# Decaying attention with a soft mixture of experts on one core: fill transposes left out, the first pair of tiles reordered, two steps of the softmax moved

## The chip, the cores and the metric

One core of one Trainium2 chip. The metric is the device time of the slowest (here the only) core in microseconds, lower is better. The kernel before takes 162.74 us, the median of three runs (161.5, 162.74 and 279.86).

## The reference

Two stages, all in float32. The first is causal attention with a decay and no softmax, for 4 batches, 8 heads, 768 positions and 64 channels; `lam` is one number per head:

```python
intra = (q_b @ k_b.T * Dmask) @ v_b          # Dmask[i, j] = lam ** (i - j) for i >= j
inter = (q_b * lam ** (pos + 1)) @ kv_state
kv_state = lam ** block * kv_state + (k_b * lam ** (block - 1 - pos)).T @ v_b
```

Its result, laid out as x of 3072 rows by 512, goes through a soft mixture of 8 experts with 4 slots each (32 slots):

```python
logits = x @ phi                              # 3072 x 32
slot_input = softmax(logits, over rows).T @ x # 32 x 512
slot_out[e] = relu(slot_input[e] @ w1[e]) @ w2[e]   # 512 -> 1024 -> 512
out = softmax(logits, over slots) @ slot_out  # 3072 x 512
```

## The kernel before

**Tiles.** The kernel cuts the positions into 24 tiles of 128 (6 per batch, so a block is 128 positions here, which is the same sum) and works on pairs of tiles, u = 0 to 11 (line 497). Head h is numbered by hp (4) and hh (2): the two halves of a pair of heads lie in partitions 0 to 63 and 64 to 127. The engines run through lists written out by hand: the wrapper `InOrder` (line 39) keeps every instruction in program order on its engine, so the order of the Python calls is the order on each engine, and the profile puts every instruction at line 49. The lines below are those of the source.

**Pair u.** `scores` (209) multiplies K by Q into the banks sc0 and sc1 for the first tile and tr and dp for the second; `masked` (224) multiplies each bank by the decay mask on VectorE (tile `at`). `turn_k` (246) turns the next two tiles' K by PE transposes into the banks xa and xb, and copies them to `kn`: the first bank on VectorE, with the decay `kpow` multiplied in, the second on ScalarE without. For the heads of the second bank `decay_v` (266) multiplies V by the decay on GpSimd instead (tile `vd`). `gathered` (326) makes the new K-by-V state in bank kv, `carry` (345) adds the old one on VectorE (`st`), `decay_state` (357) multiplies it by the decay on GpSimd (`dec`), and `decay_q` (230) prepares the decayed Q (`qs`). `recall` (287) and `attend` (302) sum the output of both tiles in xa and xb, and ScalarE copies it to `xt`. `natural` (363), called at the head of the next pair (510), turns `xt` back by PE transposes into tr and dp and copies the two banks to `x`, both on ScalarE. So tr and dp are free for the scores of the pair's second tile only when the copies are done.

**Softmax.** Every second pair ends with `logits` (376), a generator that runs up to each `yield`: the matmul of four tiles with phi (bank gl), the maximum `mx` and the negative running maximum `nm` on VectorE, and the exponential `e` on ScalarE before the first `yield`; `alpha` before the second; the copy `L` before the third; the sum `lsum` before the fourth. In odd pairs two steps run at the end (570 and 572), the others behind `recall` in the next pair (541, 542). `weights` (412) transposes e and L on PE, `slots` (444) sums the weighted rows, `slot_softmax` (420) makes the second softmax in the meantime.

**Loads.** All loads go through SyncE's queue in the order of the program: 14 buffers for the inputs, which come free as the matmuls read them, and between them the 32 slabs of w1, at the pace that the constants AHEAD and PACE set (`feed`, 87). The w2 tiles (`w2t`, later the pairs `w2p`) follow into buffers that the attention has left and into slabs whose w1 has been used.

**The experts, in two parts.** `first` (666) multiplies by w1, `second` (704) by w2. `second(0)` makes the left half of the 512 columns in bank kv (line 769), `second(1)` the right half in bank xa (line 789), 16 items of four multiplications each (`quad`, 693; each shows as two matmul instructions in the profile, so an item is x8). Between the items of `second(1)` the table `fill` runs other work: `spread(0)` ahead of item 1, `last_C` ahead of item 2, and `put(0..2, 0)` ahead of items 3, 5 and 7, which makes the left half of the output and sends it off in 12 transfers of 256 KB (tensor y). Ahead of items 9 to 15 runs `still` (782):

```python
    def still():
        nonlocal top
        top = bank("xb")
        idle(5)

    for n in range(AT_IDLE, 16):
        fill[n] = still
```

`idle` (589) transposes the identity into a bank that nobody reads. After `second(1)` a copy (`so`), `spread(1)` and three `put` make the right half, another 12 transfers.

Of the kernel before, what the change touches and what calls it, by code (L numbers as in the profile page):

```python
# [8 lines left out]
F32 = mybir.dt.float32  # L9
F32R = mybir.dt.float32r  # L10
AF = mybir.ActivationFunctionType
ALU = mybir.AluOpType
AX = mybir.AxisListType

P = 128
B, H, S, DH = 4, 8, 768, 64
NB = S // P
T = B * NB
HP = H // 2
# [11 lines left out]

AT_SPREAD = 1
AT_PUTS = (3, 5, 7)
AT_IDLE = 9
AHEAD = 30
PACE = 29

# [17 lines left out]
def decay_attn_soft_moe(  # L55
# [13 lines left out]
    pe, dve, act, pool, sp = (InOrder(tc, x) for x in (nc.tensor, nc.vector, nc.scalar, nc.gpsimd, nc.sync))  # L69
# [4 lines left out]
    work = ctx.enter_context(tc.tile_pool(name="work", bufs=1))  # L74
# [4 lines left out]
    def bank(tag):  # L79
        return ps.tile([P, 512], F32, tag=tag, name=tag)  # L80
# [5 lines left out]
    IN = {}  # L86
# [75 lines left out]
    for hh in range(2):  # L162
        for hp in range(HP):
            x = hh * HP + hp
            dve.tensor_tensor_scan(
                out=mask[:, hh, hp, :],
# [22 lines left out]
    kpow = mask.rearrange("p a b i -> p (a b) i")[:, :, P - 1:P]  # L189
    CN = const.tile([P, T, SL], F32, name="CN")  # L190
    acc = const.tile([P, D], F32, name="acc")
    lsum = const.tile([P, 1], F32, name="lsum")
# [50 lines left out]
                k = slice(DH * r, DH * r + DH)  # L243
                pe.transpose(dst[r][:, i * DH:(i + 1) * DH], x[k], ident[k, k])

    def turn_k(ts, tags):

        ts = [t for t in ts if has_state(t)]
        if not ts:
            return  # L250
        tk = [bank(tag) for tag in tags]
        turn(tk, [IN[t, 1][:, hp * P:(hp + 1) * P] for t in ts for hp in range(HP)])
        n = len(ts)
        kn = [work.tile([P, 2, HP, DH], F32, tag="kn", name="kn", bufs=2) for _ in range(2)]
        tk = [x[:, 0:n * HP * DH].rearrange("p (i h c) -> p i h c", i=n, h=HP) for x in tk]
        dve.tensor_tensor(
            out=kn[0][:, 0:n],
            in0=tk[0],
            in1=kpow[:, 0:HP].rearrange("p (o h) x -> p o h x", o=1).broadcast_to([P, n, HP, DH]),
            op=ALU.mult,  # L260
        )
        act.copy(out=kn[1][:, 0:n], in_=tk[1])
        for i, t in enumerate(ts):
            KN[t] = kn[0][:, i], kn[1][:, i]

    def decay_v(ts):
        ts = [t for t in ts if has_state(t)]
        if not ts:
            return
        vd = work.tile([P, 2, HP, DH], F32, tag="vd", name="vd")  # L270
        for i, t in enumerate(ts):
            v_ = IN[t, 2].rearrange("p (h c) -> p h c", h=H)
            pool.tensor_tensor(
                out=vd[:, i],
                in0=v_[:, HP:H],
                in1=kpow[:, HP:H].broadcast_to([P, HP, DH]),
                op=ALU.mult,
            )
            VD[t] = v_[:, 0:HP], vd[:, i]
# [7 lines left out]
    def recall(t, opens):  # L287

        qs, st = QS.pop(t), ST[t - 1]
        for hp in range(HP):  # L290
            for hh in range(2):
                r = slice(64 * hh, 64 * hh + 64)
                pe.matmul(
                    out=place(t, hh, hp),
                    lhsT=st[r, hp, :],
                    rhs=qs[r, hp, :],
                    start=(opens and hp < 2),
                    stop=True,
                    skip_group_check=True,
                )  # L300
# [62 lines left out]
    def natural(ts, tags, copies):  # L363
        tr = [bank(tag) for tag in tags]
        turn(tr, [XT[t][:, hp, :] for t in ts for hp in range(HP)])
        x = keep.tile([P, 2, D], F32, tag="x", name="x", bufs=2)
        y = x.rearrange("p i (g r c) -> p r (i g) c", r=2, c=DH)
        for r in range(2):
            copies[r](out=y[:, r], in_=tr[r].rearrange("p (g c) -> p g c", c=DH))
        for i, t in enumerate(ts):  # L370
            X[t] = x[:, i]
# [4 lines left out]
    def logits(g):  # L376
        pl = bank("gl")
        for hp in range(HP):
            for c in range(4):
                pe.matmul(  # L380
                    out=pl[SL * c:SL * c + SL, 0:P],
                    lhsT=phi_sb[:, hp, :],
                    rhs=XT[4 * g + c][:, hp, :],
                    start=(hp == 0),
                    stop=(hp == HP - 1),
                )
        pl = pl[:, 0:P]
        mx = small.tile([P, 1], F32, tag="mx", name="mx")
        dve.tensor_reduce(out=mx, in_=pl, axis=AX.X, op=ALU.max)
        new = small.tile([P, 1], F32, tag="nm", name="nm")  # L390
        old = run.get("m")
        if g == 0:
            dve.tensor_scalar(out=new, in0=mx, scalar1=-1.0, scalar2=None, op0=ALU.mult)
            act.activation(out=e, in_=pl, func=AF.Exp, bias=new, scale=1.0, accum_out=lsum)
        else:
            dve.scalar_tensor_tensor(out=new, in0=mx, scalar=-1.0, in1=old, op0=ALU.mult, op1=ALU.min)
            rs = small.tile([P, 1], F32, tag="rs", name="rs")
            act.activation(out=e, in_=pl, func=AF.Exp, bias=new, scale=1.0, accum_out=rs)
        run["m"] = new
        yield  # L400
        if g > 0:
            alpha = small.tile([P, 1], F32, tag="alpha", name="alpha")
            act.activation(out=alpha, in_=old, func=AF.Exp, bias=new, scale=-1.0)
            run["alpha"] = alpha
        yield
        act.copy(out=L, in_=pl)
        yield
        if g > 0:
            dve.scalar_tensor_tensor(out=lsum, in0=lsum, scalar=alpha, in1=rs, op0=ALU.mult, op1=ALU.add)
        yield  # L410
# [84 lines left out]
    ask = sm = late_sums = iter(())  # L495
    kvs = [None]
    for u in range(NU):
        a, b, c = 2 * u, 2 * u + 1, 2 * u + 2
        opens, last = a % NB == 0, u == NU - 1
        feed(u)  # L500
        if u == NU - 2:
            for _ in range(NLOAD - 6):
                load_one(*ld1)
        if last:
            for tag, n in (("kn", 2), ("vd", 1)):
                for _ in range(n):
                    load_one(work, tag, n)

        if u > 0:
            natural((a - 2, a - 1), ("tr", "dp"), (act.copy, act.copy))  # L510
            carry(a, kvs[0][:, 1])
            decay_state(a)
            turn_k((b, c), ("xa", "xb"))
        scores(a, ("sc0", "sc1"))
        masked(a, 0)
        masked(a, 1)
        if u == 0:
            decay_v((0,))
            decay_q(1)
            turn_k((0,), ("xa", "xb"))  # L520
            scores(b, ("tr", "dp"))
        xb = [bank("xa"), bank("xb")]
        XB[a], XB[b] = (xb, 0), (xb, 2 * P)
        if u == 0:
            kv = gathered((0,))
            carry(0, kv[:, 0])
            decay_state(0)
            masked(b, 0)
            masked(b, 1)
            turn_k((b, c), ("sc0", "sc1"))  # L530
            decay_v((b, c))
            decay_q(c)
            recall(b, True)
        else:
            scores(b, ("tr", "dp"))
            masked(b, 0)
            masked(b, 1)
            if not opens:
                recall(a, True)
            recall(b, opens)  # L540
            next(ask, None)
            next(ask, None)
            next(late_sums, None)
            decay_v((b, c))
            if u == 1:
                place_phi()
            decay_q(c)
            if u % 2 == 0:
                sm = slot_softmax(u // 2 - 1, weights("gl"))
                next(sm)  # L550
            decay_q(c + 1)
        xt = keep.tile([P, 2, HP, P], F32, tag="xt", name="xt", bufs=2)

        def states():
            kvs[0] = gathered((b, c))
            carry(b, kvs[0][:, 0])
            decay_state(b)

        attend((a, b), xt, states if u % 2 == 0 else None)
        next(sm, None)  # L560
        if u == 0:
            constants()
        if u % 2 == 1 and not last:
            states()
        if u == 0:
            decay_q(c + 1)
        next(sm, None)
        if u % 2 == 1:
            ask = logits(u // 2)
            next(ask)  # L570
            if not last:
                next(ask)
        elif u > 0:
            late_sums = slots(u // 2 - 1)
            next(late_sums)
# [13 lines left out]
    def idle(n):  # L589

        for _ in range(n):
            pe.transpose(top[:, 0:P], ident, ident)
# [185 lines left out]
    fill = {AT_SPREAD: lambda: spread(0), AT_SPREAD + 1: last_C}  # L778
    for i in range(3):
        fill[AT_PUTS[i]] = lambda i=i: put(i, 0)  # L780

    def still():
        nonlocal top
        top = bank("xb")
        idle(5)

    for n in range(AT_IDLE, 16):
        fill[n] = still
    second(1, po1, fill)
    act.copy(out=so[:, HD:D], in_=po1[:, 0:HD])  # L790
    spread(1)
# [59 lines left out]
```

## Time and profile before

| | us |
|---|---|
| median of the runs | 162.74 (161.5, 162.74, 279.86) |
| the profiled execution | 161.27 |
| its span, first to last instruction | 159.5 |
| PE busy | 147.2 (92%) |
| VectorE, ScalarE, GpSimd busy | 80.6, 50.3, 51.3 |
| mean granted TensorE clock | 0.982 |
| moved by DMA | 59.18 MB, 371 GB/s over the span |

The span runs from the first to the last instruction; the profiled execution took 1.77 us more than its span. PE's busy time has modelled ends, so that short pauses between matmuls don't show in it, and a chain of waits has to be read beside it. A DMA share a little above 1 means that all 16 engines were busy.

### The profile page before, as it was taken

The page shows a single profiled execution, that of the slowest core. Times are in us where ns is not written, and L with a number is a line of the kernel's source. Part 1 is how long each engine was busy: PE and PEld are TensorE (multiplying, and loading weights), DVE is VectorE, ACT ScalarE, POOL GpSimd, SP SyncE. Part 2 cuts the span into 40 slices and gives each one's busy share as a digit, 9 for nine tenths or more (in the row PEclk, how much of TensorE's full clock was granted, in tenths as well). Part 3 has the DMA queues.
Part 4 walks back from the last instruction along what each step waited for, and adds up shares of the span by engine and source line. Part 5 has one row for each costly group of instructions (what it writes and reads, how often), then busy time and mean ns, then how long its engine had stood idle before and what let it go on. Part 6 is the DMA issues. An engine that isn't in the chain of part 4 may idle for free.

```text
span 159.5 us, 6104 instructions
## 1 busy us (share of the span) xinstructions
PE 147.2 (92%) x2614; PEld 109.4 (69%) x2614; DVE 80.6 (51%) x180; ACT 50.3 (32%) x116; POOL 51.3 (32%) x74
## 2 busy tenths in 40 slices
PE   8968999999999999999999999899999999997900
PEld 8957998789879987997789878753234645553500
DVE  0975727384957394848584966363314006300720
ACT  3012334434433453334434532430101035201610
POOL 1168683572662286553562660001000000000000
PEclk9999999999999999999999999999999999999975
DMA  5999999999999999999999999999999999991496
GB/s 170 351 396 409 412 406 408 412 389 360 402 401 398 405 401 406 410 398 394 369 398 379 420 403 394 384 395 382 401 408 408 399 408 399 387 352 41 163 384 242
DMA packets 30714, 59.18 MB, mean 371 GB/s; under 512 B 2912, under 2 KB 9184, under 8 KB 30688
## 3 DMA queue, kind: packets, MB, share of 16 engines
q1 hardware_dynamic: 30544, 58.80, 96.9%
q8 instruction: 20, 0.33, 0.7%
q14 instruction: 6, 0.05, 0.1%
q10 hardware_dynamic: 144, 0.01, 0.1%
HBM read 52.50 MB, written 6.29 MB: 369 GB/s over the span
## 4 chain that ended last, share of the span: by engine, by line
PE 87%; DVE 3%; DMA 2%; ACT 2%; issue 1%; DVEq 1%
PE xa L49 24%; PE xb L49 14%; PE gl L49 12%; PE kv L49 12%; PE tr L49 11%; PE sc L49 9%; PE dp L49 5%; DMA lam_sb<-lam_x 2%; DVE mask L49 2%; DVE qpow L49 1%; DVE at L49 1%; DVEq L847 1%; ACT so L49 0%; ACT xt L49 0%; ACT o L49 0%
## 5 line engine op out<-in xcount | busy, mean ns | idle before, releaser
L49 POOL TENSOR_TENSOR qs<-ld,qpow 128x512 f32<-128x512 f32 x20 | 25.3, 1277 | 10.3 <-issue 5.3
L49 DVE TENSOR_TENSOR at<-sc,mask 128x512 f32<-128x512 f32 x24 | 15.4, 684 | 5.1 <-PE sc L49 5.1
L49 POOL TENSOR_TENSOR vd<-ld,mask 128x256 f32<-128x256 f32 x20 | 12.4, 623 | 14.8 <-DMA ld<-vN 9.7
L49 POOL TENSOR_TENSOR dec<-st,qpow 128x256 f32<-128x256 f32 x16 | 10.0, 623 | 14.5 <-DVE st L49 10.8
L49 PE MATMUL tr<-ld 64*128 64x128 f32 x96 | 14.5, 281 | 0.0
L49 PE MATMUL sc<-ld 64*128 64x128 f32 x192 | 14.3, 292 | 0.0
L49 PE MATMUL dp<-ld 64*128 64x128 f32 x96 | 13.5, 280 | 0.0
L49 PE MATMUL xa<-at,ld 128*64 128x128 f32 x192 | 13.4, 280 | 0.0
L49 PEld LDWEIGHTS sc<-ld 64*128 64x128 f32 x192 | 12.5, 200 | 0.2 <-issue 0.2
L49 ACT COPY xt<-xa 128x512 f32<-128x512 f32 x12 | 6.9, 578 | 18.1 <-PE xa L49 18.1
L49 PE MATMUL xb<-at,ld 128*64 128x128 f32 x192 | 12.6, 273 | 0.0
L49 PE MATMUL kv<-ld,kn 128*64 128x64 f32 x160 | 11.4, 222 | 1.2 <-DVE kn L49 1.2
L49 PEld LDWEIGHTS dp<-ld 64*128 64x128 f32 x96 | 11.6, 187 | 1.1 <-ACT x L49 1.1
L49 DVE TENSOR_TENSOR st<-dec,kv 128x256 f32<-128x256 f32 x16 | 6.6, 414 | 11.3 <-PE kv L49 9.8
L49 PEld LDWEIGHTS tr<-ld 64*128 64x128 f32 x96 | 12.1, 187 | 0.2 <-ACT x L49 0.2
L49 PEld LDWEIGHTS kv<-ld,kn 128*64 128x64 f32 x160 | 10.8, 138 | 1.7 <-DVE kn L49 1.7
L49 PEld LDWEIGHTS xa<-at,ld 128*64 128x64 f32 x192 | 10.2, 136 | 2.3 <-DVE at L49 1.2
L49 PE MATMUL xb<-qs,st 64*64 64x128 f32 x160 | 11.4, 277 | 0.0
L49 PE MATMUL xa<-qs,st 64*64 64x128 f32 x160 | 11.4, 276 | 0.0
L49 PE MATMUL kv<-vd,kn 128*64 128x64 f32 x160 | 11.3, 222 | 0.0
L49 PEld LDWEIGHTS tr<-ident,xt 64*128 64x128 f32 x96 | 6.9, 139 | 6.1 <-ACT xt L49 4.7
L49 PEld LDWEIGHTS kv<-vd,kn 128*64 128x64 f32 x160 | 10.8, 138 | 0.0
(154 smaller groups left out, 328.1 us busy)
## 6 DMA issues: line engine op xcount, KB each, us to landing
slab<-w_x SPq DMA_DIRECT2D x32, 512.0 KB, 6.8
w2p<-w_x SPq DMA_DIRECT2D x20, 512.0 KB, 10.2
ld<-kT SPq DMA_DIRECT2D x24, 256.0 KB, 5.4
ld<-qT SPq DMA_DIRECT2D x24, 256.0 KB, 5.2
ld<-vN SPq DMA_DIRECT2D x24, 256.0 KB, 6.1
w2t<-w_x SPq DMA_DIRECT2D x24, 256.0 KB, 5.2
y<-o SPq DMA_DIRECT2D x24, 256.0 KB, 3.8
L<-phi_x SPq DMA_DIRECT2D x1, 64.0 KB, 4.3
```

Of the source, the lines that this page charges most:

```text
L49: return self._tc.keep_in_program_order(f(*args, **kwargs))
L847: with tile.TileContext(nc) as tc:
```

## The change

- `still` is left out, with its seven entries in the table `fill`: `second(1)` runs items 9 to 15 with nothing between them.
- In pair 0 `turn_k` copies both banks on ScalarE, without the decay (`raw`), and `decay_first` multiplies V of tile 0 by the decay for all eight heads on GpSimd, in one instruction over 128x512 in place of one over 128x256.
- In `logits` a `yield` stands ahead of the exponential `e`. It is asked for at the head of the even pairs, behind the copies of `natural`; `alpha`, `L` and `lsum` follow behind `recall`. After the last pair the order is as before.
- At the head of a pair, `carry` and `decay_state` stand ahead of `natural`; `natural` copies its second bank on VectorE. In pair 1 `turn_k` stands ahead of `natural`, in the later pairs behind it (and behind `e`).

```diff
--- before.py
+++ after.py
@@ -31,7 +31,6 @@
 
 AT_SPREAD = 1
 AT_PUTS = (3, 5, 7)
-AT_IDLE = 9
 AHEAD = 30
 PACE = 29
 
@@ -243,7 +242,7 @@
                 k = slice(DH * r, DH * r + DH)
                 pe.transpose(dst[r][:, i * DH:(i + 1) * DH], x[k], ident[k, k])
 
-    def turn_k(ts, tags):
+    def turn_k(ts, tags, raw=False):
 
         ts = [t for t in ts if has_state(t)]
         if not ts:
@@ -253,15 +252,28 @@
         n = len(ts)
         kn = [work.tile([P, 2, HP, DH], F32, tag="kn", name="kn", bufs=2) for _ in range(2)]
         tk = [x[:, 0:n * HP * DH].rearrange("p (i h c) -> p i h c", i=n, h=HP) for x in tk]
-        dve.tensor_tensor(
-            out=kn[0][:, 0:n],
-            in0=tk[0],
-            in1=kpow[:, 0:HP].rearrange("p (o h) x -> p o h x", o=1).broadcast_to([P, n, HP, DH]),
-            op=ALU.mult,
-        )
+        if raw:
+            act.copy(out=kn[0][:, 0:n], in_=tk[0])
+        else:
+            dve.tensor_tensor(
+                out=kn[0][:, 0:n],
+                in0=tk[0],
+                in1=kpow[:, 0:HP].rearrange("p (o h) x -> p o h x", o=1).broadcast_to([P, n, HP, DH]),
+                op=ALU.mult,
+            )
         act.copy(out=kn[1][:, 0:n], in_=tk[1])
         for i, t in enumerate(ts):
             KN[t] = kn[0][:, i], kn[1][:, i]
+
+    def decay_first():
+        vd = work.tile([P, 2, HP, DH], F32, tag="vd", name="vd")
+        pool.tensor_tensor(
+            out=vd.rearrange("p a h c -> p (a h) c"),
+            in0=IN[0, 2].rearrange("p (h c) -> p h c", h=H),
+            in1=kpow.broadcast_to([P, H, DH]),
+            op=ALU.mult,
+        )
+        VD[0] = vd[:, 0], vd[:, 1]
 
     def decay_v(ts):
         ts = [t for t in ts if has_state(t)]
@@ -391,12 +403,13 @@
         old = run.get("m")
         if g == 0:
             dve.tensor_scalar(out=new, in0=mx, scalar1=-1.0, scalar2=None, op0=ALU.mult)
-            act.activation(out=e, in_=pl, func=AF.Exp, bias=new, scale=1.0, accum_out=lsum)
+            rs = lsum
         else:
             dve.scalar_tensor_tensor(out=new, in0=mx, scalar=-1.0, in1=old, op0=ALU.mult, op1=ALU.min)
             rs = small.tile([P, 1], F32, tag="rs", name="rs")
-            act.activation(out=e, in_=pl, func=AF.Exp, bias=new, scale=1.0, accum_out=rs)
         run["m"] = new
+        yield
+        act.activation(out=e, in_=pl, func=AF.Exp, bias=new, scale=1.0, accum_out=rs)
         yield
         if g > 0:
             alpha = small.tile([P, 1], F32, tag="alpha", name="alpha")
@@ -507,17 +520,22 @@
                     load_one(work, tag, n)
 
         if u > 0:
-            natural((a - 2, a - 1), ("tr", "dp"), (act.copy, act.copy))
             carry(a, kvs[0][:, 1])
             decay_state(a)
-            turn_k((b, c), ("xa", "xb"))
+            if u == 1:
+                turn_k((b, c), ("xa", "xb"))
+            natural((a - 2, a - 1), ("tr", "dp"), (act.copy, dve.tensor_copy))
+            if u % 2 == 0:
+                next(ask)
+            if u > 1:
+                turn_k((b, c), ("xa", "xb"))
         scores(a, ("sc0", "sc1"))
         masked(a, 0)
         masked(a, 1)
         if u == 0:
-            decay_v((0,))
+            decay_first()
             decay_q(1)
-            turn_k((0,), ("xa", "xb"))
+            turn_k((0,), ("xa", "xb"), True)
             scores(b, ("tr", "dp"))
         xb = [bank("xa"), bank("xb")]
         XB[a], XB[b] = (xb, 0), (xb, 2 * P)
@@ -540,6 +558,7 @@
             recall(b, opens)
             next(ask, None)
             next(ask, None)
+            next(ask, None)
             next(late_sums, None)
             decay_v((b, c))
             if u == 1:
@@ -568,7 +587,7 @@
         if u % 2 == 1:
             ask = logits(u // 2)
             next(ask)
-            if not last:
+            if last:
                 next(ask)
         elif u > 0:
             late_sums = slots(u // 2 - 1)
@@ -778,14 +797,6 @@
     fill = {AT_SPREAD: lambda: spread(0), AT_SPREAD + 1: last_C}
     for i in range(3):
         fill[AT_PUTS[i]] = lambda i=i: put(i, 0)
-
-    def still():
-        nonlocal top
-        top = bank("xb")
-        idle(5)
-
-    for n in range(AT_IDLE, 16):
-        fill[n] = still
     second(1, po1, fill)
     act.copy(out=so[:, HD:D], in_=po1[:, 0:HD])
     spread(1)
```

## Rows read from the trace of the kernel before

**Rows 1.** The page: GB/s in 40 equal slices of 3.99 us

```profile
GB/s 170 351 396 409 412 406 408 412 389 360 402 401 398 405 401 406 410 398 394 369 398 379 420 403 394 384 395 382 401 408 408 399 408 399 387 352 41 163 384 242
```

**Rows 2.** Stretches: PE, PEld, DVE, ACT, POOL busy; clock; DMA share; GB/s

```profile
142.00:144.00 2.00, 2.00 (x25) 0.95 (x22) 0.00 (x0) 0.00 (x0) 0.00 (x0) 1.00 0.83 290
...
146.00:148.00 2.00, 1.51 (x24) 0.99 (x27) 0.00 (x0) 0.37 (x1) 0.00 (x0) 1.00 0.00 0
...
148.00:150.00 2.00, 1.73 (x26) 1.20 (x22) 1.53 (x3) 1.41 (x3) 0.00 (x0) 1.00 0.10 36
...
156.00:158.00 2.00, 0.00 (x0) 0.00 (x0) 0.00 (x0) 0.00 (x0) 0.00 (x0) 0.50 1.08 382
```

**Rows 3.** The chain that ended last, part two: start, us, what

```profile
120.94 6.95 PE kv L49 x128
...
135.58 1.00 PE xa L49 x16
...
136.58 0.70 PE xb L49 x5
...
137.28 0.57 PE xa L49 x8
...
145.51 0.38 ACT so L49
```

**Rows 4.** Transfers of y and w2p: issues, then size and us to landing

```profile
148.89 6.88 SPq L49 DMA_DIRECT2D y<-o  x12
...
L49 SPq DMA_DIRECT2D w2p<-w_x x20: 367/613/982, 106.3 to 126.5; - x20
...
w2p<-w_x SPq DMA_DIRECT2D x2, 512.0 KB, 10.4
```

**Rows 5.** Timeline of the first pair, 6 to 12 us, by engine

```profile
6.36 0.65 POOL L49 TENSOR_TENSOR vd<-ld,mask 128x256 f32<-128x256 f32 x1 [5.03 <-DVE mask L49]
...
7.99 1.27 POOL L49 TENSOR_TENSOR qs<-ld,qpow 128x512 f32<-128x512 f32 x1 [0.99 <-DVE qpow L49]
...
7.27 0.37 ACT L49 COPY kn<-xb 128x256 f32<-128x256 f32 x1 [4.63 <-PE xb L49]
...
7.84 1.26 DVE L49 TENSOR_TENSOR at<-sc,mask 128x512 f32<-128x512 f32 x2
...
9.48 0.27 PE L49 MATMUL kv<-ld,kn 128*64 128x64 f32 x1 [1.22 <-DVE kn L49]
...
11.35 1.20 POOL L49 TENSOR_TENSOR vd<-ld,mask 128x256 f32<-128x256 f32 x2
```

**Rows 6.** Issue of tile 2's V at 5.89 us: us to landing

```profile
ld<-vN SPq DMA_DIRECT2D x1, 256.0 KB, 5.3
```

**Rows 7.** The chain in pairs 6 (55.87) and 7 (64.13)

```profile
55.87 0.95 PE sc L49 x16
...
58.19 0.25 PE xa L49
...
64.13 0.95 PE sc L49 x16
...
65.97 0.25 PE xa L49
```

**Rows 8.** Timeline of pair 6, ACT and DVE

```profile
55.38 0.37 ACT L49 ACTIVATE e<-gl,nm 128x128 f32<-128x128 f32 x1 [1.49 <-PE dp L49]
...
56.39 0.59 ACT L49 COPY x<-dp 128x512 f32<-128x512 f32 x1
...
55.91 0.69 DVE L49 TENSOR_TENSOR kn<-xa,mask 128x512 f32<-128x512 f32 x1 [0.29 <-PE xb L49]
...
56.86 1.29 DVE L49 TENSOR_TENSOR at<-sc,mask 128x512 f32<-128x512 f32 x2 [0.26 <-PE sc L49]
```

**Rows 9.** Stretches in which PE had pauses: columns as in rows 2

```profile
8.00:9.00 1.00, 0.25 (x5) 0.06 (x2) 1.00 (x2) 0.00 (x0) 1.00 (x1) 1.00 1.01 383
...
153.50:154.00 0.50, 0.00 (x0) 0.00 (x0) 0.00 (x0) 0.00 (x0) 0.00 (x0) 0.63 1.10 385
```

## The prediction

> **What bounds the kernel now.** I read the page's slices first, then the stretches at the end, then the chain that ended last, and only then single engines. The slices show that the transfers run at some 400 GB/s from 8 us up to 140 us, and that they stop once: 41 GB/s in the slice at 143.5 us [rows 1]. The stretches place the hole. At 142 to 144 us 290 of the 382 GB/s that the stream of y reaches are left, at 146 to 148 us there is nothing, and at 148 to 150 us some 0.2 us' worth [rows 2]. So the stream of weights and of the left half of y is used up at about 142 + 2 x 290/382 = 143.5 us (143.7 with a rest behind it), the right half begins at about 149.8 us, and between them lie 6.1 us without transfers. In them the chain is PE's: items of `second(1)` with five transposes ahead of each, up to the copy `so` at 145.51 us [rows 3]. From the first issue of the right half at 148.89 us [rows 4] to the end of the span are 10.6 us, and they are transfers at 382 GB/s, not work of an engine [rows 2].
>
> There are thus two limits that I carry along: PE's chain, which says when the right half can start, and the sum of the transfers, which says when it can end at the earliest. With the hole closed the transfers end at 159.5 - 6.1 = 153.4 us.
>
> **The fills of part two.** Seven times five transposes with 0.70 us, and behind each an item with 0.57 us: 7 x 1.27 = 8.89 us of the chain [rows 3]. Items that follow each other directly need less: 16 of them took 6.95 us in `second(0)`, 0.434 us each [rows 3]; two together took 1.00 us ahead of the fills. The lower bound is the transposes alone, 7 x 0.70 = 4.9 us, the upper one 8.89 - 7 x 0.434 = 5.85 us. I take 5.8 us, because the seven items will stand as the sixteen did. What is late next? The items need their w2p. The last of these is issued at 126.5 us and lands 10.4 us later, at 136.9 us [rows 4]; the last two items would begin at 136.58 + 5 x 0.434 = 138.75 us. So 1.9 us of slack are left, and no wait arises as long as the rest of the kernel stays where it is. PE's chain alone gives 159.5 - 5.8 = 153.7 us of span, just behind the 153.4 us of the transfers. No queue is crossed: the transposes issue no transfer, and nobody reads their bank.
>
> **The first pair.** PE waits 1.22 us for `kn` of tile 0, which on VectorE stands behind two masks (7.84 to 9.10 us) [rows 5]. On ScalarE, which has been idle for 4.63 us, it is a second copy of 0.37 us behind the one at 7.27 us, done at about 8.0 us. The product with V now covers 512 columns; the same kind of instruction of that size took 1.27 us, against 0.65 us for the half [rows 5]. From 6.36 us it ends at 7.63 us, ahead of `qs` at 7.99 us, so it is hidden; uncovered it would cost 0.6 us. The gain is at most PE's 1.22 us. The other end is V of tile 2: issued at 5.89 us and landing after 5.3 us [rows 6], it allows its product of 0.6 us from 11.2 us, ready at 11.8 us, where the two products now end at 12.55 us [rows 5]: 0.7 us. I take 0.9 us.
>
> **Pair 1, with `turn_k` ahead.** Its transposes write xb, and xb is free only after the same copy to `xt` for which `natural` waits. The two only swap behind one wait: 0. Its sixteen short transposes are about half a stage of 0.95 us [rows 7], so the bounds are -0.5 and +0.5 us.
>
> **The copies and e.** In pair 6 the scores of the second tile take from 55.87 + 0.95 = 56.82 to 58.19 us, 1.37 us; in pair 7, from 65.08 to 65.97, 0.89 us [rows 7]. The difference, 0.48 us, is a wait for bank dp: ScalarE takes e first, then the first copy, then at 56.39 us the second, which ends at 56.98 us [rows 8]. Worked out in the same way, seven of the eleven pairs have such a loss (0.54, 0.48, 0.23, 0.48, 0.73, 0.48 and 0.48 us in pairs 2, 4, 5, 6, 8, 10 and 11), 3.42 us together. With e behind, and the second bank on VectorE beside the first on ScalarE, dp is free before the scores of the first tile end. Behind e on ScalarE now stands only the copy of `kn`, and `alpha` and `L` behind that; L is wanted only after `recall`, so this is hidden. VectorE pays: one more copy (about 0.69 us, the price of its 128x512 `kn` [rows 8], some 0.6 us where the next follows) ahead of `kn` and the masks. There it idles 0.29 + 0.26 = 0.55 us, waiting for PE [rows 8], so the masks come some 0.1 us later at worst. Pair 6 opens a batch, has only half of the `recall` between the scores and `attend`, and there the masks hold about half of the gain back. I take 3.0 us. The bounds are 3.4 us, and a loss of 0.6 us if the masks are each time late by that 0.05 to 0.1 us and PE gains nothing.
>
> **The sum.** PE's chain becomes 5.8 + 0.9 + 3.0 = 9.7 us shorter, and would give 149.8 us of span. But the transfers don't become fewer; they end at 153.4 us less what the loads move ahead. That is the term that decides. Against 407 GB/s, the level of good slices, the 32 slices from 8 to 136 us lack 2.65 us' worth [rows 1]; the six slices under 390 GB/s alone (at 32, 36, 76, 84, 100 and 108 us) lack 1.75 us. In part one a load waits for its buffer, which PE frees; with PE 1 to 4 us earlier these waits shrink. Bounds 0 and 2.65 us; I take 1.2 us, two thirds of the deep holes. So the span is 153.4 - 1.2 = 152.2 us, and the execution 152.2 + 1.77 = 154.0 us. The profiled execution with its 161.27 us lies 0.2 us under the lower and 1.5 us under the higher of the two timed runs that agree with it; I add the 0.2 us: **154.2 us**. Of the 9.7 us of PE, some 2.4 us then end as waiting for w2p and in the queue of y.
>
> **The rivals.** Over 2% faster means under 159.5 us, and 2% is about what a measurement of this kernel can tell from no change.
>
> *The early edits give nothing.* Then PE's chain and the transfers end nearly together, at 153.7 us: 155.6 us. For it: VectorE has just 0.55 us of room, and V of each pair arrives late. Against it: the same wait in seven pairs. 0.22.
>
> *The loads fill all their holes.* 153.4 - 2.65 = 150.8 us, as an execution 152.7 us. For it: PE is ahead everywhere. Against it: not every weak slice is a wait for a buffer. 0.18.
>
> *VectorE becomes the bound of part one.* Its copy costs 0.61 us in eleven pairs, 6.7 us, if nothing hides it: 161.27 + 6.7 - 5.8 = 162.2 us, the same time as before. Against it: the 0.55 us that VectorE idles there. 0.05.
>
> *TensorE falls to half its clock in part two.* The fills kept PE occupied; without them it may wait for w2p between items. With PE idle at the end, the row at 153.5 us shows a granted clock of 0.63, in passing from 2.4 to 1.2 GHz; on the other side PE was busy for only a quarter of the stretch at 8 us and kept 1.00 [rows 9]. If the clock fell at the start of part two, PE's work from the end of `second(0)` at 127.9 us to `so`, 17.6 - 5.8 = 11.8 us, and 1.5 us behind it [rows 2, 3] would double: 161.27 - 5.8 + 13.3 = 168.8 us, slower. It decides from the point where more than 5.8 us of this work are left, at about 135.4 us (4.3 us ahead of the new `so`); later than that the doubled rest is within what was saved. Against it: `second(0)`, without fills, held its 0.434 us for sixteen items [rows 3], and the wait that I expect, 3.9 us of PE earlier less 1.9 us of slack and 1.2 us of loads, is 0.8 us, as long as the pause at 8 us. 0.05.
>
> The Trainium skill speaks for this rival: "TensorE: Matmul & The Clock Gate", section "HAM oscillation — how this bites in real kernels", has kernels lose half the clock each time that PE waits for a transfer between short groups of matmuls. By that rule the time would be the 168.8 us; the trace so far bears it out only for the end of the kernel, where no matmul follows.
>
> **How the numbers follow.** The forecast has 0.50, the rivals 0.22, 0.18, 0.05 and 0.05. Its own range, with 0 to 2.4 us of loads moved ahead, is 153.0 to 155.4 us. To take in most of the first two rivals I give 152.3 to 156.4 us. Faster by over 2%: 0.50 + 0.22 + 0.18 = 0.90; within 2%: 0.05, VectorE; slower: 0.05, the clock.
>
> **What would show it.** The chain should show the last seven items in some 3.0 to 4 us, and `so` not later than 139.7 us. The slices should show no hole at 143 us, and the y of the right half should take longer to land than now, since it queues behind the left half. The first `gathered` should start near 8.3 us, and the scores of the second tile take 0.9 us in every pair. A hole that stays would say that PE's chain still sets the end, and masks that hold `attend` would say that VectorE gave the gain back. A granted clock under 1.00 ahead of 150 us makes the prediction wrong, and so do slices under 380 GB/s all through part one.

## The result and the profile after

The changed kernel takes 156.4 us (median of 155.38, 155.83, 156.96 and 157.36), the kernel before 162.74 us in the same runs (161.5, 162.74 and 163.62); the ratio is 0.9616, with a 95% interval of 0.9499 to 0.9734. A second measurement gave 155.17 us against 161.62 us, 0.9569 (0.9497 to 0.964). An execution that took over 1.5% longer than the fastest of its kernel is left out of all medians, ranges and ratios here: 279.86 us of the kernel before, two executions each of fills and less_both, one each of late_put and hold.

So the change makes the kernel some 4% faster. The forecast, 154.2 us, counts from 161.5 us for the kernel before, a ratio of 0.955, which lies in both intervals; taken against the median of 162.74 us it is 0.948 and lies just under both. It was 1.0 and 2.2 us too low, and 156.4 us stands at the very end of the stated range (as a ratio, 156.4/162.74 = 0.961, the measured 0.9616 is just beyond it).

Two profiled executions of the changed kernel differ enough to be read side by side: the first took 157.36 us (span 155.6), the second, called after_again below, 154.58 us (span 152.8). The transfers of the first, in 40 slices of 3.89 us, and PE's granted clock in tenths, which answer to [rows 1]:

```profile
PEclk9959999999999999999999999999999999999955
...
GB/s 159 354 385 354 404 390 404 403 401 400 404 407 408 407 401 410 411 406 413 408 407 409 407 409 390 332 337 382 325 403 408 409 401 407 403 383 383 383 384 127
```

And of the second, in slices of 3.82 us, with a clock line that has 9 in each of its first 38 slices:

```profile
GB/s 164 358 402 410 409 405 410 408 409 406 405 384 394 403 401 416 404 405 411 410 409 399 390 416 394 386 382 400 398 395 409 406 404 408 402 384 380 335 383 201
```

The hole at 143.5 us is gone in both: from 8 us to the end of y the transfers run on. In the second a dip to 335 is left of it, at 141 us. The first has three weak stretches that the second hasn't: 354 at 12 us, and 332, 337 and 325 between 97 and 113 us. And its clock falls to 5 tenths at 8 us.

The chain of part two, second execution; it answers to [rows 3]:

```profile
119.58 6.95 PE kv L48 x128
...
126.55 0.38 ACT so L48
...
138.31 0.38 ACT so L48
```

From the end of `second(0)` to the right half's `so` are 11.76 us; before they were 17.59 us (127.92 to 145.51). The fills are worth 5.83 us, as worked out. In the first execution the same stretch took 12.34 us, because PE waited 0.5 us for w2p, and its chain runs at that place not through PE but through a transfer of the left half, up to 140.50 us. Its chain, and below it the right half's `so` on ScalarE's timeline, since the chain doesn't pass it:

```profile
120.05 6.95 PE kv L48 x128
...
133.12 7.38 DMA y<-o
```

```profile
139.37 0.37 ACT L48 COPY so<-xa 128x256 f32<-128x256 f32 x1 [3.59 <-PE xa L48]
```

The scores of the second tile in pair 6, which took 1.37 us [rows 7], now follow without a pause, 56.54 to 57.43 us (first execution):

```profile
55.59 0.95 PE sc L48 x16
...
57.43 0.25 PE xa L48
```

**Where the time went.** Three terms, each against the profile before (span 159.5 us), make up the two spans exactly:

| | first | second | forecast |
|---|---|---|---|
| start of `second(0)`, before at 120.94 us | 120.05: -0.89 | 119.58: -1.36 | -3.9 |
| from there to `so` of the right half, before 24.57 us | 19.32: -5.25 | 18.73: -5.84 | -5.8 |
| from `so` to the end, before 13.99 us | 16.23: +2.24 | 14.49: +0.50 | +2.4 |
| span | -3.9 | -6.7 | -7.3 |

The last column's +2.4 us is what I had put down as waiting for w2p and in the queue of y. The fills came out as forecast; the tail grew by 2.2 us in the first execution, nearly as forecast, and by only 0.5 us in the second; of PE's early gain of 3.9 us 0.9 and 1.4 us came. The limit differs too: in the first execution the transfers don't weaken from 113 us to the end of y, in the second they dip once, where the right half begins.

### The profile page after: what moved, and what is told of

Its sections match the earlier page's. It is cut to its first block, busy times and chain, and to the rows that moved or that the text cites. A ratio compares the mean times of both kernels' runs of the same rounds, so it can differ in the third digit from the quotient of the medians.

```text
span 155.6 us, 6026 instructions
## 1 busy us (share of the span) xinstructions
PE 139.8 (90%) x2579; PEld 105.4 (68%) x2579; DVE 86.8 (56%) x190; ACT 45.3 (29%) x106; POOL 51.8 (33%) x74
## 4 chain that ended last, share of the span: by engine, by line
PE 81%; DMA 8%; ACT 2%; SPq 1%; issue 1%; DVEq 1%; DVE 0%
PE xa L48 20%; PE tr L48 14%; PE gl L48 12%; PE kv L48 12%; PE xb L48 11%; PE sc L48 9%; DMA y<-o 5%; DMA ld<-kT 3%; PE dp L48 2%; SPq L48 1%; DVEq L858 1%; ACT xt L48 0%; ACT o L48 0%; ACT e L48 0%; DVE o L48 0%
## 5 line engine op out<-in xcount | busy, mean ns | idle before, releaser
L48 POOL TENSOR_TENSOR vd<-ld,mask 128x256 f32<-128x256 f32 (+1 forms) x20 | 12.8, 645 | 16.0 <-DMA ld<-vN 10.8
L48 PE MATMUL tr<-ld 64*128 64x128 f32 x96 | 13.7, 286 | 1.7 <-DMA ld<-kT 1.7
L48 PE MATMUL sc<-ld 64*128 64x128 f32 x192 | 13.8, 279 | 0.3 <-issue 0.3
L48 PEld LDWEIGHTS sc<-ld 64*128 64x128 f32 x192 | 11.9, 189 | 0.6 <-issue 0.5
L48 PEld LDWEIGHTS dp<-ld 64*128 64x128 f32 x96 | 12.3, 198 | 0.0
L48 PE MATMUL kv<-vd,kn 128*64 128x64 f32 x168 | 12.0, 232 | 0.0
L48 DVE COPY x<-dp 128x512 f32<-128x512 f32 x12 | 8.2, 687 | 5.9 <-PE dp L48 5.9
L48 PE MATMUL kv<-ld,kn 128*64 128x64 f32 x152 | 10.8, 222 | 0.5 <-issue 0.5
L48 ACT COPY x<-tr 128x512 f32<-128x512 f32 x12 | 7.0, 586 | 14.4 <-PE dp L48 12.4
```

Source lines behind the costliest of these rows:

```text
L48: return self._tc.keep_in_program_order(f(*args, **kwargs))
```

## The experiments

Times below are medians over the executions of a kernel, with their range behind them; single executions of one kernel differ by 1 to 2 us, so I lean on profiles, of one execution each, where a few tenths matter.

**Which part is worth what.** `after_again` is the changed kernel. The three others undo parts of it:

```diff
# fills: as before, but
-    for n in range(AT_IDLE, 16):
-        fill[n] = still
# fills_copies: as changed, but
-            decay_first()
+            decay_v((0,))
-            turn_k((0,), ("xa", "xb"), True)
+            turn_k((0,), ("xa", "xb"))
# fills_start: as changed, but natural, carry, decay_state, turn_k and e as before
```

> The changed kernel once more, as the mark for its variants. If the late start of its first pair (scores of pair 1 at 17.22 us against 16.40 us before, with a granted clock of 0.5 from 8 to 11 us) belongs to the new order, it is there again and the time is 156.4 us within 1 us. If it was one execution's luck, the first pair runs at clock 1.00, pair 1 starts its scores before 15.9 us, and the time is 155.4 us or less.

> Only the fill transposes left out; the first pair, the copies of x and e as before. If PE's chain sets the end, 5.8 us less than the kernel before: 155.5 us, a ratio of 0.964. If the sum of the transfers sets it, 155.2 us, the same. If the early edits are worth the 2.2 us that PE gained between pairs 1 and 8, this kernel is 1 to 2 us slower than the changed one; if their gain is given back in the stream of transfers, it is as fast.

> The fills left out and the copies of x and e moved; the first pair as before. If the new first pair costs time (0.8 us late in the profile of the changed kernel, where 0.9 us of gain were forecast), this one is 1 to 1.7 us faster than the changed kernel, near 155 us, and its pair 1 starts at 16.4 us. If the stream of transfers sets the end whatever happens early, it is the same within 0.5 us.

> The fills left out and the first pair reordered; copies of x and e as before. If the copies of x are worth what the chain shows (2.1 us of the seven waits for bank dp are gone), this one is about 2 us slower than the changed kernel. If the loads of V and the late weights hold PE and the stream, it is the same within 0.5 us.

Measured medians: 155.17 us (154.58 to 155.99), 156.24 (155.53 and 156.95), 155.92 (155.19 to 157.09) and 157.0 us (156.86 to 159.16); before 161.62. The fills alone give a ratio of 0.9631 (0.952 to 0.9742) of the 0.9569; fills_copies has 0.9618 (0.9538 to 0.9697), and fills_start 0.9719 (0.9614 to 0.9824), not clear of 2%. The copies and e are worth 0.3 us on top of the fills and 1.8 us on top of fills and first pair; the first pair costs 0.8 us without them and gains 0.8 us with them. Differences of this size are within the spread, so the early edits can't be priced from these times. The late start of the first profile was that execution's own: after_again starts pair 1 at 15.81 us, with a full clock.

**Are the early edits worth 3.9 us of PE?** With the fills put back PE's chain sets the end again:

```diff
+    for n in range(AT_IDLE, 16):
+        fill[n] = still
```

> The changed kernel with its seven fills put back, so that PE's chain sets the end of part two again. If the early edits bring PE to part two 1.4 us earlier, as the second profile of the changed kernel has it, 1.4 us less than the kernel before: 160.2 us. If they bring the 3.9 us that I forecast for PE, 157.7 us. If they bring nothing, 161.6 us.

Measured: 160.23 us (159.95 to 161.7) against 161.53 us, 0.9889 (0.9831 to 0.9948): 1.3 us, under 2%. Its profiled execution is the slowest of the five, 161.7 us. Then the same question with slack in the transfers, in the kernel before and in the changed one:

```diff
+                if len(wt) < 4:
                     t_ = slabs.tile([P, 2, 512], F32, tag="slab", name="slab")
                     sp.dma_start(out=t_, in_=w1[4 * Q + q, kc])
+                else:
+                    t_ = wt["w1", 0, q, 0]
                 wt["w1", Q, q, kc] = t_
```

> The kernel before, with only 4 of the 32 slabs of w1 loaded and used for all (14.7 MB less in part one), so that the transfers have slack there. If PE sets the pace of part one and not the loads, the pairs keep their period of 7.95 us: from the scores of pair 1 to those of pair 11 79.5 us, as now. If the loads hold it, it is shorter.

> The changed kernel with the same cut. If the saturated transfers took the gain of the copies (late loads, or late instructions of PE, whose pauses in the middle of a group come with them), the seven waits for bank dp now count in full: from pair 1 to pair 11 3 us shorter than in the kernel before with the same cut, and no pause inside a group of matmuls. If PE gives the gain back for a reason of its own (masks on VectorE), it stays at 0.4 to 0.6 us and the pauses stay.

They took 161.64 and 153.45 us, one execution each. The scores of pairs 1 and 11 and `second(0)` in the chain, kernel before with the cut:

```profile
16.48 0.95 PE sc L49 x16
...
96.27 0.95 PE sc L49 x16
...
121.28 6.95 PE kv L49 x128
```

and changed kernel with the cut:

```profile
15.73 0.95 PE sc L48 x16
...
92.94 0.95 PE sc L48 x12
...
117.61 6.95 PE kv L48 x128
```

From pair 1 to pair 11 are 79.79 us before and 77.21 us after, 2.58 us less; `second(0)` starts 3.67 us earlier, where 3.9 us were forecast. With all transfers the same two stretches, in the kernel before and in after_again, are 79.52 us and 79.11 us, 0.41 us less, and `second(0)` starts 1.36 us earlier:

```profile
16.40 0.95 PE sc L49 x16
...
95.92 0.95 PE sc L49 x16
```

```profile
15.81 0.95 PE sc L48 x16
...
94.92 0.95 PE sc L48 x16
```

So the edits do to PE nearly what was worked out, and with all transfers two thirds of it are lost. The share is that of one execution of each kernel: in the profiles that have both early edits and all loads `second(0)` starts between 118.9 us (late_put) and 121.36 us (early_only).

**By which way?** after_again and light_after have the same list for PE, and their scores start together up to pair 4 (38.97 and 38.99 us). Pair 5 starts 0.75 us later in after_again (47.70 against 46.95 us), pair 9 1.51 us (79.20 against 77.69 us), and pair 11 1.98 us; `second(0)` has 1.97 us. So 1.8 us are lost in pairs 4, 8 and 10 alone, and not a little in each pair, as late loads would have it. In these three pairs PE pauses inside groups of matmuls, where no new data is waited for. The scores of pair 4 in the timeline of after_again:

```profile
38.81 0.88 PE L48 MATMUL sc<-ld 64*128 64x128 f32 x10
...
39.98 0.60 PE L48 MATMUL sc<-ld 64*128 64x128 f32 x5 [0.29 <-issue]
```

Ten of sixteen, then a pause of 0.6 us (39.4 to 39.98 us), and a releaser that the profile doesn't name. early_only and, further below, less_pe, less_both and k_first pause at the same place, behind the tenth, by up to 1.1 us. The first execution of the changed kernel has no pause there, but 0.47 us in pair 8 (up to 75.99 us) and 0.29 us in pair 10 (up to 88.22 us). The two light kernels have none at pair 4, and light_after has none inside a group anywhere. A list that is fetched in pieces would do that. So six instructions were added ahead of it:

```diff
             turn_k((0,), ("xa", "xb"), True)
+            still = bank("gl")
+            for _ in range(6):
+                pe.transpose(still[:, 0:P], ident, ident)
```

> The changed kernel, with six transposes of the identity (bank gl, not read) behind the first turn_k of pair 0, where PE waits for K of tile 1. If PE's pauses inside a group of matmuls are its own instructions arriving late, in pieces that begin at fixed places of its list, they move: in pair 4 from behind the 10th matmul of the scores to behind the 4th, and in pair 8 six matmuls earlier too. If they are waits for data, they stay where they are or vanish. The time stays within 0.5 us of the changed kernel (155.2 us), or falls by up to 0.5 us if the six keep the clock up in the first pair.

Pair 4 in this kernel:

```profile
38.90 0.44 PE L48 MATMUL sc<-ld 64*128 64x128 f32 x4
...
39.56 0.94 PE L48 MATMUL sc<-ld 64*128 64x128 f32 x12 [0.21 <-issue]
```

Four, then the pause: it moved by the six instructions that were added. Pair 8's pause, behind the ninth matmul of `gathered` in after_again (75.2 to 75.75 us), doesn't show there any more, and one in the scores of pair 10 moved from behind the 14th (as the chain places it) to behind the 8th, again by six. So these are places in PE's list, not places where data is missing.

PE's own instructions arriving late fits this. The page's part on the queues has their transfers, in queue q8: 20 packets with 0.33 MB. In after_again packets start at 37.63, 73.35 and 85.48 us, and PE goes on after its three pauses at 39.98, 75.75 and 87.75 us, 2.3 to 2.4 us later. In all 13 profiles that have such pauses between pairs 1 and 11 (31 in all, over 0.3 us from one matmul's start to the next in the same group, without the step of 0.43 us that the matmuls with x have in every kernel), PE goes on 2.2 to 2.5 us after a packet's start. In hold the packet of pair 8 starts at 71.94 us, and the place that the pause would have moved to is reached at 74.4 us, 2.5 us later: nothing is left to wait for. The profile names no releaser, so this is as near as the traces come.

That the packets are late because the transfer engines are full of loads is inferred from the light kernels. light_before's PE runs as that of the kernel before, but the 11th to 15th packets start at 71.0, 77.8, 85.0, 88.9 and 94.5 us, with all loads at 73.3, 78.7, 85.3, 91.3 and 96.1 us. after_again has them at 73.4, 79.3, 85.5, 91.5 and 96.4 us, no earlier than the kernel before, though its PE is 1 us ahead: PE catches up with its own list. The kernel before, whose PE still waits for dp, has none of these pauses, with all loads or without, and fills has none. What starts a packet isn't shown, and no run changes the fetch alone. The time of hold, 155.63 us (154.95 to 156.32; ratio 0.9618), isn't better: keeping PE at work in the first pair for six transposes longer gains nothing.

**Which of the two moves freed dp?**

```diff
# e_old
-            if u % 2 == 0:
-                next(ask)
...
-            if last:
-                next(ask)
+            next(ask)
# act_copies
-            natural((a - 2, a - 1), ("tr", "dp"), (act.copy, dve.tensor_copy))
+            natural((a - 2, a - 1), ("tr", "dp"), (act.copy, act.copy))
```

> The changed kernel with e asked for at the end of the odd pairs again; VectorE still copies the second bank of x. If the second copy's move to VectorE alone frees bank dp, the scores of the second tile still take 0.89 us in every pair. If e in front of the first copy matters too, bank tr is late in the even pairs instead, and these scores take 0.2 to 0.5 us more there.

> The changed kernel with both banks of x copied by ScalarE again, e still behind them. If e was what made bank dp late, the scores of the second tile take 0.89 us in the even pairs, since the second copy ends 0.5 us earlier than in the kernel before. If it is the second copy as such, pairs 5 and 11 keep their waits of 0.23 and 0.48 us (no e stands there), and the even pairs have none or a small one.

155.29 us (0.9604, 0.9555 to 0.9653) and 155.3 us (0.9607, 0.9559 to 0.9654): the same as both moves together. In the timelines e_old has the scores of the second tile without a wait in pairs 3 to 10, and 0.7 us of wait in pair 2; act_copies has none in pairs 3, 4, 6, 7 and 9, some 0.2 us in pairs 2, 5, 8 and 10, 0.47 us in pair 11 and 0.5 us in pair 1. So VectorE's copy alone is enough but for one pair, and e behind is enough in most; together they count once. Each first expectation held, with these exceptions.

**What sets the end?**

```diff
# less_bytes: the last four tiles of w2 (two w2p) not loaded
-    while late:
+    while len(late) > 4:
         load_two()
+    while late:
+        Q_, f_, q_ = late.pop()
+        wt["w2", Q_, q_, f_] = wt["w2", Q_, q_, f_ - 1]
# less_pe
+        todo = todo[:12] if part else todo
# less_both: both
```

> The changed kernel, but the last two w2p (1 MB, 2.6 us of the stream) are not loaded; items 14 and 15 use the w2 of items 12 and 13 in their place. If the transfers alone set the end, 2.6 us less than the changed kernel (155.2 us): 152.6 us. If PE's chain alone sets it, the same 155.2 us. If both end nearly together, as the forecast had it, 0.5 to 0.8 us less.

> The changed kernel, but items 12 to 15 of the second part are left out (1.74 us of PE); all loads stay. If PE's chain alone sets the end, 153.5 us. If the transfers alone set it, the same 155.2 us. If both end nearly together, up to 0.5 us less.

> Both cuts together: items 12 to 15 left out and 1 MB of w2 not loaded. If both limits end nearly together, only this one is clearly faster than the changed kernel, by 1.7 to 2.2 us. If the transfers alone set the end, 2.6 us, as with the bytes alone; if PE alone, 1.74 us, as with the items alone.

Measured: 154.05 us (153.84 to 154.25), 156.38 us (155.57 to 157.22) and 153.04 us (152.51 and 153.56), ratios 0.9516, 0.9661 and 0.9453. Taking 1.74 us of PE away gives nothing; taking 2.6 us of transfers away gives 1.1 us and brings the hole back. The stretch at 140 us has 381 GB/s in less_pe, and in less_bytes (columns: length, busy time of PE, its weight loads, VectorE, ScalarE and GpSimd, granted clock, DMA share, GB/s):

```profile
140.00:142.00 2.00, 1.77 (x30) 1.31 (x32) 0.96 (x2) 1.00 (x2) 0.00 (x0) 1.00 0.22 75
```

So the transfers set the end, and the limit that PE sets lies about 1 us below theirs. Both cuts together give 2.1 us less than after_again, as expected if both limits end nearly together (1.7 to 2.2 us), but from two executions that lie 1 us apart; this third one is not settled.

**Two tries to get further.**

```diff
# late_put: fill has put(0, 0) and put(1, 0) only
     spread(1)
+    put(2, 0)
     for i in range(3):
         put(i, 1)
# k_first: the order of the first loads
-    for t, i in ((0, 1), (0, 0), (0, 2), (1, 0), (1, 1), (1, 2)):
+    for t, i in ((0, 1), (0, 0), (1, 1), (1, 0), (0, 2), (1, 2)):
```

> The changed kernel, with the third put of the left half moved from ahead of item 7 to behind the second part, so that the right half can start about 1 us earlier and the left half's last four transfers bridge the gap. If a short hole between the halves is what PE still costs at the end, 0.3 to 0.5 us less than the changed kernel (155.2 us). If the transfers are closed already, no difference.

> The changed kernel, with K of tile 1 loaded ahead of V of tile 0, 0.65 us earlier. If PE's wait for that K is what lets the clock fall in some executions and starts pair 1 late, the times come closer together and 0.3 to 0.8 us lower on average, with no granted clock under 1.00 ahead of 140 us. If the spread comes from the transfers later on, no difference.

155.57 us (0.9635, 0.9607 to 0.9664) and 155.74 us (0.9658, 0.9601 to 0.9716): no gain. late_put's `so` comes 1 us earlier (137.33 us), but its left half has fewer transfers in the queue, and the hole only moves (276 GB/s in the slice at 138 us). With k_first pair 1 starts at 15.53 us, 0.3 us earlier, and the executions still spread from 155.22 to 157.3 us: the wait for K is not what makes them differ. No version that does all of the work beats the changed kernel.

## Why the prediction was right and wrong

**Fills: right.** 5.83 us against 5.8 us, and the transfers of the two halves meet, as worked out. The rival that TensorE falls to half its clock in part two did not come: 1.00 up to 146 us in both executions, and the waits for w2p were 0.5 and 0.2 us. (The pause at 8 us that I likened to a wait of 0.8 us is 1.22 us long in [rows 5].) The clock fell at another place, and in one execution only. In the first one PE stands still from 6.2 to 7.9 us, waiting for K of tile 1, and the granted clock (third column from the end) falls:

```profile
6.00:7.00 1.00, 0.18 (x6) 0.04 (x2) 1.00 (x4) 0.65 (x2) 0.44 (x1) 1.00 0.97 322
...
8.00:9.00 1.00, 1.00 (x11) 1.00 (x13) 1.00 (x3) 0.00 (x0) 0.37 (x1) 0.52 1.06 404
```

Half speed, 1.2 GHz, in the stretch from 8 us, and pair 1 starts at 17.22 us. In after_again the same wait is 0.86 us long and the clock stays at full speed; but it stays so in fills_start and early_only too, where the wait is 1.70 and 2.00 us long and PE is busy for only 0.30 and 0.27 us between 6 and 8 us (0.29 us in the first execution). So the pause alone doesn't decide it, and what does stays open. The rule of the Trainium skill on pauses for transfers ("TensorE: Matmul & The Clock Gate", section "HAM oscillation — how this bites in real kernels") is borne out here in one execution and not in the two others.

**First pair: too high.** The chain gained 0.59 us at pair 1 (15.81 against 16.40), not 0.9 us. I had called GpSimd's longer product hidden. It is off PE's path, but it lies beside VectorE's four scans of `qpow`, and holds one of them. The second scan before:

```profile
6.50 0.78 DVE L49 TENSOR_TENSOR_SCAN qpow<-lam_sb,zero 128x128 f32<-128x128 f32 x1
```

and in after_again:

```profile
6.63 1.21 DVE L48 TENSOR_TENSOR_SCAN qpow<-lam_sb,zero 128x128 f32<-128x128 f32 x1
```

0.43 us more; the other three take 0.39 to 0.40 us each in both, and behind the four stand the masks. In every profile but one the scan that starts within the product ends 0.28 us behind the product's end. So all four take 1.72 to 1.73 us in the four profiles with a product of 256 columns (0.64 to 0.79 us), and 2.16 to 2.19 us where one of 512 (1.06 to 1.08 us) starts within the first scan. In k_first the product starts later, at 7.36 us, when the last scan has already begun; none is held, and the four take 1.34 us. So the product beside them is the price, and not the data. The first `gathered` then starts at 7.83 us in after_again (8.3 us were forecast), but what it gains waits for the masks.

**Copies and e: right in kind, wrong in size.** This is the step that failed: "PE's chain becomes 5.8 + 0.9 + 3.0 = 9.7 us shorter". The waits for dp went (0.89 us in nearly all pairs), but of the 0.9 + 3.0 = 3.9 us of both early edits only 1.4 us reached part two in the second execution and 0.9 us in the first; early_only has 1.3 us. With fewer loads 3.67 us reach it. Between after_again and light_after lie 1.97 us at `second(0)`, 1.8 us of them lost at three places of PE's list, which fits instructions that come late while the transfers are saturated. I had the transfers as a limit of the end only, not as one of PE's pace in part one.

**Loads moved ahead: right in size, not in every execution.** Adding up the slices at 128 us, the stream of after_again is 1.4 us ahead of the one before, that of e_old 1.3, of act_copies and hold 1.2, of k_first 1.0, of late_put 0.9, of fills_copies 0.6, of less_pe 0.4 and of fills_start 0.3 us, and that of fills 0.2 us behind; I had taken 1.2 us ahead. In the first execution it is 1.1 us behind: 0.6 us lost up to 16 us, and what it had made up by 88 us (0.8 us ahead) lost between 96 and 112 us (the slices of 332, 337 and 325 GB/s above). So in the execution of 157.36 us it is this term of the transfers, "they end at 153.4 us less what the loads move ahead", that failed, by 2.3 us; their stream has no hole at the end there, so what PE lost did not add to it. Why they were slow is open. early_only's profile has the like at another place: 322 and 314 GB/s between 44 and 52 us, and 1.1 us behind at 128 us.

**The sum** had no term for PE being late at the end and none for the spread. With PE's gain at 1.4 us the right half starts 2.5 us later than in the sum, just late enough to leave a hole of 0.5 us in the good execution. And I set the level by the profiled execution before, 161.27 us, the fastest of its kind then. The executions of the changed kernel lie between 154.6 and 157.4 us, 2.8 us apart, for which my own range of 153.0 to 155.4 us had no room. VectorE did not become the bound (86.8 us busy of 155.6), and the rival that the early edits give nothing, priced at 155.6 us, was the nearest to the medians of 155.2 and 156.4 us, but by luck: they did give PE 1.3 us, and the spread made up the rest.

## What to carry to other kernels

Where transfers fill every slice, a gain on an engine is worth only what the stream lets it keep, and the engine's own instructions come with that stream: work out for each stretch which of the two has slack, and test it once with fewer bytes. Two profiles of the same list, laid side by side pair by pair, then show where the time goes. Filler work on the chain can be priced from a stretch of the same work without it, and comes out as priced. A product moved to GpSimd is not free because GpSimd idles; look at which VectorE instruction starts beside it.

## What I had not expected of the hardware

PE's own instructions seem to come late when the transfers are saturated: pauses of 0.3 to 1.1 us inside a group of matmuls, at a fixed place of the list, which moved by six when six instructions were put ahead, and which end 2.2 to 2.5 us after an instruction packet's start. And a GpSimd product of 1.08 us over 512 columns held the one VectorE scan that started beside it until 0.28 us after its own end, 1.21 us in place of 0.40 us.
